# An attention and max-of-three FFN kernel: the row maximum turned by two 64-row matmuls, key totals folded in blocks, FFN products freed from one chain, a new order

## The chip, the cores and the metric

One Trainium2 chip, one of its cores. The metric is the device time of one execution in microseconds. Each version is also run once under the profiler, which records each instruction of each engine. Five engines matter: TensorE (PE, with its weight loads as PEld), VectorE (DVE), ScalarE (ACT), GpSimd (POOL), and SyncE (SP), which here only issues DMAs.

## The reference

```python
# q, k, v: (8, 8, 1152, 64) float32; x @ w: (4608, 512) @ (512, 768), w_out: (768, 512)
q_pool = q.reshape(B, H, S // 2, 2, D).mean(axis=3)
scores = np.matmul(q_pool, k.transpose(0, 1, 3, 2)) / np.sqrt(D)
scores = scores - np.max(scores, axis=-1, keepdims=True)
attn = np.exp(scores)
attn = attn / (np.sum(attn, axis=-1, keepdims=True) + 1e-09)
x = np.matmul(attn, v).transpose(0, 2, 1, 3).reshape(B * 576, H * D)
out = np.maximum(np.maximum(x @ w1, x @ w2), x @ w3) @ w_out
```

## The kernel before

**Units.** The attention is cut into 64 units d: a batch, a pair of heads and half of the 576 queries (288). Keys lie on the 128 partitions in nine blocks kk. Each unit does, in short:

1. qk (L568, L581): each key block times the queries of both heads, one head on array rows 0 to 63, the other on rows 64 to 127, into one of two PSUM slots `pqk`. From unit 8 on, K and Q are split into a high and a low part, and each product is three passes. ACT copies the slot to SBUF `s` (L597), and DVE takes the running maximum `acc` over key blocks (L603, L606).
2. The maximum over the partitions: DVE turns and reduces `acc` by 32 by 32 blocks to 18 columns of `crest` (L642), PE transposes `crest` whole, 128 by 128 (L652), DVE reduces it to 18 rows (L656), ACT and DVE split it into a high and a low part (L661, L664), POOL spreads both into block diagonals `diag` (L667), and two matmuls with ones, one for each head, broadcast the maximum over partitions into PSUM (L691).
3. DVE subtracts it from `s` (L703, six instructions a unit), ACT takes the exponential (L711), and POOL adds the nine key blocks into `ksum` (L743, L745).
4. av (L772): `s` times `v`, 36 matmul records a unit, one head on array columns 0 to 63, the other on 64 to 127. ACT copies the result to `xr` (L781).
5. The totals, from unit 8 on: `total` (L787) multiplies a matrix of ones with `ksum`, so that the sum stands on all partitions of its head; ACT adds 1e-9 (L791), DVE takes 288 reciprocals a partition (L795), POOL scales `xr` (L798). The first eight units use another form (L820 to L857). ACT and POOL then split x into `xh` and `xl` (L909, L912).

**FFN.** Ten chunks of token columns (288, 288, six of 512, 384, 576). A chunk makes 18 weight tiles g (three per hidden block of 128), each with four products kk, each of three passes (L1053); then four output tiles, each with six products. `two` makes two output tiles together: phase 0 puts the first tile on rows 0 to 63 and the second on rows 64 to 127, phase 1 changes the halves over. A tiny ACT copy, the mark (L1074), waits for the last matmul of phase 0, and the first matmuls of phase 1 wait for the mark. All products lie on one chain, `tail[0]`. Each tile goes from PSUM to SBUF `hm` (ACT copy L1114 for the first of three, DVE maximum L1116 for the second and third), and then ACT and POOL split `hm` into `h` high and low (L1124, L1127). The first output product waits for all of `h`.

**PSUM.** Four banks `ff` are shared by the FFN tiles (two for each call of `two`), the turned and the broadcast maxima, av and the totals. `spool` holds THIRDS = 7 thirds of a unit's `s`.

**Order.** Each `step` is an entry of a plan in the order of its creation. `ORDER` lists the entries' numbers, and `run` emits them in that order, so that every engine's queue is what `ORDER` says. The plan's own costs (`pe`, `act`, `dve`, `pool`) do nothing when the kernel is run. A step's `after` are steps that must be emitted earlier.

Of the kernel before, what the change touches and what calls it, by code (L numbers as in the profile page):

```python
# [24 lines left out]
NB = 18  # L25
DM = 512
# [11 lines left out]
1 3 68 0 2 7 9 8 10 12 11 13 14 4 333 5 342 15 18 16 17 21 65 67 334 19 337 335 20 336 24 338 66 22 343 25 339 23 27  # L38
28 26 344 30 31 29 70 32 72 346 71 73 340 33 34 75 345 35 36 76 74 77 37 78 132 351 910 352 353 347 38 81 79 80 354 46
39 84 355 82 83 87 40 51 348 85 88 41 86 90 89 93 911 133 130 6 195 356 52 131 349 360 197 42 91 94 92 95 96 44 43 357  # L40
135 137 136 138 139 140 97 143 45 141 47 144 142 145 98 146 149 48 361 147 99 49 100 196 358 101 912 148 150 151 362
54 152 363 50 53 153 154 102 155 109 55 158 364 198 369 341 69 267 706 264 365 56 156 370 112 366 115 113 159 110 157
103 373 111 160 161 200 201 57 202 162 205 58 203 104 105 163 371 164 206 114 106 204 165 207 372 107 208 59 209 367
166 707 374 211 212 174 167 116 375 108 175 265 376 134 266 350 378 387 210 60 213 61 168 170 119 178 176 214 217 215
180 120 218 379 382 169 216 219 220 223 121 221 224 172 62 63 380 222 225 269 271 381 388 391 226 389 383 390 177 173
270 272 384 171 122 392 385 123 227 274 273 64 228 229 230 277 275 278 124 393 179 276 708 543 199 774 709 396 377 231
279 184 232 239 280 233 240 775 394 241 245 283 281 284 181 397 234 125 185 235 282 286 287 285 398 126 127 399 288
289 186 128 292 405 400 401 243 237 406 290 187 402 293 409 236 242 291 407 188 294 295 296 408 403 189 297 298 410
117 129 299 300 247 248 711 713 712 714 359 386 368 414 268 777 253 715 246 244 308 301 716 313 717 719 254 190 309
# [12 lines left out]
891 581 944 582 945 946 947 837 948 583 1145 481 1212 478 1146 838 949 1147 950 584 839 479 892 1148 480 951 1150 840
899 585 952 1151 953 841 954 1149 1210 487 885 1216 1152 488 489 900 893 894 895 1215 1213 896 482 955 963 1153 956
901 903 964 957 966 968 1156 483 490 586 1211 1217 491 965 492 958 902 484 493 1154 1157 1155 590 1158 959 591 592
1159 1162 593 904 967 1160 905 1161 1163 594 595 1165 960 1166 1164 906 907 961 1167 1168 908 596 597 598 1169 1170
1221 1223 969 962 599 1171 1172 909 600 1173 1345 588 495 923 467 503 980 601 589 485 602 1347 970 971 972 973 587 974
975 496 504 1174 1222 1218 499 1224 507 497 498 1175 505 1176 506 1225 1177 1178 603 604 1226 1180 500 508 981 501
1227 605 606 607 1179 1182 1228 1229 1184 1230 509 1181 608 609 610 611 1232 1231 612 1185 502 1219 976 510 977 1235
618 619 620 621 1233 1236 1186 1234 1238 615 622 1187 1237 511 623 624 625 626 1239 1240 1189 1241 1188 512 515 1244
1242 1348 627 513 616 617 631 519 632 1346 633 634 635 636 1245 613 1183 637 1190 1243 1283 1284 1246 514 1247 638  # L70
1285 1286 1191 1192 1193 1194 614 516 1248 1288 639 640 628 1249 1250 520 629 1251 1252 1195 517 518 1196 494 1220
1287 521 522 1291 1253 641 1289 527 642 523 644 645 1199 1254 1256 1258 1290 643 1352 1354 1200 1255 524 1257 525 1259
1201 1205 1260 1261 1292 1206 646 1294 1295 647 648 649 528 650 1293 1297 1298 1296 529 530 651 652 653 654 1300 1299
1303 655 1263 659 660 661 662 1262 531 1301 1350 1304 1264 663 1302 1306 1305 1265 664 1355 1353 1349 1197 526 1198
630 1267 1202 1268 532 656 658 657 1307 1266 761 982 535 983 665 666 667 1359 1360 1308 668 669 1309 1361 1275 1364
1310 536 537 1281 670 671 539 1276 1311 538 533 1312 1362 540 541 1277 1313 1363 1367 1356 1365 1366 1282 1368 534 542
1314 672 673 674 1322 675 676 677 1370 1315 678 1371 1369 1323 1325 679 680 681 682 683 684 1373 1351 1269 1270 1357
1271 1326 829 978 897 685 1374 1327 1372 1376 1316 1377 1272 762 830 898 979 1273 689 690 691 692 693 694 1318 1375
1378 1317 1319 695 1379 1382 1320 696 697 698 699 985 1483 1484 984 686 687 688 700 701 986 987 1328 988 1324 1380
1381 1421 1383 1384 1423 989 704 702 1490 1321 1385 1386 1274 1387 1278 1329 703 1337 1422 990 1424 1388 1338 991 992  # L80
993 994 995 1426 1389 1390 1425 1391 999 1000 1001 1002 1392 996 1394 1396 1429 1398 1485 1330 1331 1332 1491 1492
1003 1393 1427 1395 1004 1005 1006 1007 1339 1008 1399 1428 1401 1343 1432 998 705 1358 1011 997 1014 1015 1016 1017
1397 1486 1400 1009 1430 1433 1018 1333 1334 1335 1336 1493 1487 1013 1012 1431 1434 1403 1435 1438 1344 1436 1439
1488 1019 1020 1021 1022 1437 1441 1029 1030 1031 1032 1402 1442 1033 1440 1443 1023 1444 1445 1446 1024 1497 1498
1404 1447 1034 1035 1036 1037 1499 1502 1448 1413 1449 1340 1405 1010 1406 1407 1408 1489 1025 1038 1494 1500 1503
1039 1501 1450 1414 1451 1415 1504 1419 1028 1027 1496 1040 1621 1041 1452 1495 1409 1416 1410 1026 1453 1454 1456
1458 1042 1043 1044 1045 1505 1508 1046 1506 1509 1455 1047 1048 1049 1050 1507 1460 1511 1510 1054 1420 1512 1514
1057 1058 1051 1461 1513 1052 1515 1459 1059 1060 1061 1463 1516 1465 1517 1462 1518 1062 1063 1064 1520 1065 1056
1055 1070 1622 1071 1072 1073 1074 1075 1457 1521 1464 1519 1522 1523 1066 1559 1561 1524 1411 1623 1412 1624 1467
1468 1469 1053 1076 1560 1562 1077 1078 1564 1079 1080 1067 1525 1526 1527 1563 1466 1565 1081 1528 1567 1536 1529  # L90
1481 1566 1537 1530 1532 1534 1082 1630 1538 1626 1531 1533 1628 1568 1570 1571 1068 1482 1085 1539 1086 1087 1088
1569 1573 1475 1470 1471 1625 1472 1631 1473 1474 1629 1543 1069 1089 1541 1572 1574 1476 1627 1544 1575 1090 1091
1576 1579 1092 1093 1084 1083 1098 1099 1100 1101 1577 1580 1535 1540 1097 1102 1578 1582 1581 1635 1103 1104 1105
1106 1583 1477 1584 1094 1585 1637 1636 1640 1586 1545 1478 1546 1542 1107 1638 1641 1632 1279 1108 1280 1551 1587
1588 1552 1109 1110 1095 1557 1589 1590 1096 1633 1639 1642 1553 1547 1548 1554 1549 1930 1634 1932 1550 1931 1591
1592 1643 1558 1341 1644 1646 1647 1593 1111 1112 1645 1113 1649 1594 1648 1650 1651 1114 1598 1115 1479 1595 1599
1116 1652 1117 1653 1655 1656 1600 1654 1657 1596 1118 1119 1658 1659 1937 1597 1601 1660 1120 1121 1868 1869 1602
# [1124 lines left out]
```

## Time and profile before

| | |
|---|---|
| median of three runs | 1340.11 us (1339.11 to 1342.76) |
| the profiled execution, its own time | 1336.39 us |
| its span, first to last instruction | 1334.6 us |
| TensorE clock granted, mean | 0.994 |
| busy in the span: PE, PEld, DVE, ACT, POOL | 97%, 75%, 76%, 70%, 85% |

The page of the profile gives busy time by engine and by 40 slices, the chain of work that ended last, and the groups of instructions. Matmuls are pipelined and their ends are modelled, so that a busy PE is not a PE at its peak. Starts are microseconds from the span's first instruction.

### The profile page before, as it was taken

What the parts mean: (1) busy time and instruction counts of PE and PEld (TensorE: products, weight loads), DVE (VectorE), ACT (ScalarE), POOL (GpSimd) and SP (SyncE); (2) the same over time, 40 slices, a digit from 0 to 9 for tenths busy, and PEclk for the clock granted to TensorE, in tenths of its full rate; (3) what the DMA queues carried; (4) which work ended last, traced back from release to release, by engine and by line L of the source; (5) the groups of instructions that cost most, each with busy time, mean ns of one, the idle gap of its engine ahead of it and who ended that gap; (6) DMA issues with size and microseconds to landing.
All of it is one profiled execution on the core that took longest, in us unless ns stands there. A gap on an engine that the chain in (4) does not pass through costs nothing.

```text
span 1334.6 us, 31849 instructions
## 1 busy us (share of the span) xinstructions
PE 1293.4 (97%) x12720; PEld 997.8 (75%) x12720; DVE 1019.0 (76%) x1351; ACT 930.8 (70%) x1756; POOL 1138.3 (85%) x981
## 2 busy tenths in 40 slices
PE   6999999999999999999999999999999999999998
PEld 2556678877777777787777877778777777778887
DVE  7889998888889889888888788888887888811010
ACT  7899987687768777777777767786777876622111
POOL 3798999999999999999999999999999998772110
PEclk8999999999999999999999999999999999999999
DMA  6667775524424143324432342243341423243531
GB/s 235 204 247 258 256 263 170 198 101 147 145 86 168 51 159 123 134 83 150 147 117 86 113 179 87 70 174 105 135 167 66 144 91 146 65 158 112 167 127 37
DMA packets 56324, 189.23 MB, mean 142 GB/s; under 512 B 6128, under 2 KB 12016, under 8 KB 56176
## 3 DMA queue, kind: packets, MB, share of 16 engines
q1 hardware_dynamic: 56176, 187.20, 40.5%
q8 instruction: 100, 1.64, 0.5%
q14 instruction: 48, 0.39, 0.1%
HBM read 168.30 MB, written 18.87 MB: 140 GB/s over the span
## 4 chain that ended last, share of the span: by engine, by line
PE 59%; POOL 20%; DVE 9%; ACT 5%; issue 4%; DMA 3%; SPq 0%; POOLq 0%; ACTq 0%; DVEq 0%
PE ff L1053 32%; PE ff L772 13%; POOL ksum L745 10%; PE pqk L581 10%; DVE acc L606 4%; DVE s L703 2%; PE ff L787 2%; POOL kc L524 2%; ACT s L597 1%; POOL xl L912 1%; POOL ksum L743 1%; DMA w<-in_win_dram 1%; POOL diag L667 1%; ACT s L711 1%; PE pqk L568 1%
## 5 line engine op out<-in xcount | busy, mean ns | idle before, releaser
L745 POOL TENSOR_TENSOR ksum<-ksum,s 128x576 f32<-128x576 f32 x407 | 579.7, 1426 | 16.9 <-ACT s L711 0.6
L1053 PE MATMUL ff<-xh,w 64*128 64x512 f32 (+2 forms) x3168 | 503.4, 357 | 10.8 <-ACT flag L1074 8.8
L597 ACT COPY s<-pqk 128x576 f32<-128x576 f32 x576 | 357.7, 637 | 93.5 <-PE pqk L581 68.0
L703 DVE TENSOR_TENSOR s<-s,ff 128x864 f32<-128x864 f32 x374 | 379.7, 1047 | 28.5 <-PE ff L691 25.3
L606 DVE TENSOR_TENSOR acc<-acc,pqk 128x576 f32<-128x576 f32 x448 | 335.6, 749 | 60.8 <-ACT s L597 45.2
L711 ACT ACTIVATE s<-s 128x864 f32<-128x864 f32 x384 | 347.8, 927 | 21.5 <-DVE s L703 20.0
L1053 PEld LDWEIGHTS ff<-xh,w 64*128 64x128 f32 x3168 | 323.2, 185 | 50.3 <-ACT flag L1074 20.2
L1053 PE MATMUL ff<-xl,w 64*128 64x512 f32 (+2 forms) x1584 | 308.8, 351 | 0.0
L581 PE MATMUL pqk<-qq,kc 64*128 64x288 f32 x3024 | 296.7, 301 | 5.3 <-DVE acc L606 4.0
L772 PE MATMUL ff<-s,v 128*64 128x288 f32 x2304 | 296.4, 410 | 0.0
L581 PEld LDWEIGHTS pqk<-qq,kc 64*128 64x128 f32 x3024 | 248.6, 185 | 51.1 <-DVE acc L606 23.5
L772 PEld LDWEIGHTS ff<-s,v 128*64 128x64 f32 x2304 | 162.2, 137 | 114.9 <-issue 6.6
L1053 PEld LDWEIGHTS ff<-xl,w 64*128 64x128 f32 x1584 | 174.4, 185 | 6.7
L1116 DVE TENSOR_TENSOR hm<-hm,ff 128x512 f32<-128x512 f32 (+2 forms) x132 | 75.5, 579 | 127.4 <-PE ff L1053 96.4
L1053 PE MATMUL ff<-h,wo 64*128 64x512 f32 (+2 forms) x1584 | 169.0, 351 | 3.2 <-ACT flag L1074 2.7
L1053 PEld LDWEIGHTS ff<-h,wo 64*128 64x128 f32 x1584 | 139.6, 185 | 14.8 <-ACT flag L1074 5.3
L1127 POOL TENSOR_TENSOR h<-hm,h 128x512 fp32r<-128x512 f32 (+2 forms) x66 | 71.4, 1087 | 78.2 <-ACT h L1124 78.2
L795 DVE RECIPROCAL rs<-rs 128x288 f32<-128x288 f32 (+1 forms) x64 | 110.5, 1727 | 11.6 <-ACT rs L791 10.3
L1074 ACT COPY flag<-eps 1x1 f32<-1x1 f32 x121 | 22.7, 188 | 114.9 <-PE ff L1053 114.2
L667 POOL TENSOR_TENSOR diag<-pick,parts 64x576 fp32r<-64x576 f32 x64 | 73.8, 1152 | 22.9 <-DVE parts L664 22.1
L743 POOL TENSOR_TENSOR ksum<-s 128x576 f32<-128x576 f32 x61 | 87.6, 1436 | 2.6 <-ACT s L711 1.8
L524 POOL TENSOR_TENSOR kc<-kraw,kc 128x384 fp32r<-128x384 f32 x84 | 84.7, 1012 | 0.0
(63 smaller groups left out, 1013.1 us busy)
## 6 DMA issues: line engine op xcount, KB each, us to landing
w<-w_split SPq DMA_DIRECT2D x180, 512.0 KB, 4.5
v<-in_vr_dram SPq DMA_DIRECT2D x36, 576.0 KB, 4.9
qraw<-in_qT_dram SPq DMA_DIRECT2D x28, 576.0 KB, 4.1
kraw<-in_kT_dram SPq DMA_DIRECT2D x28, 576.0 KB, 4.3
w<-in_win_dram SPq DMA_DIRECT2D x18, 512.0 KB, 4.4
w_split<-wo SPq DMA_DIRECT2D x18, 512.0 KB, 6.8
out_dram<-hm SPq DMA_DIRECT2D x24, 256.0 KB, 2.4
w<-in_wout_dram SPq DMA_DIRECT2D x6, 512.0 KB, 4.6
```

The costliest lines, as they stand in the source:

```text
L524: nc.gpsimd.tensor_tensor(o.kc[c][:, 1], src, o.kc[c][:, 0], op=ALU.subtract)
L581: nc.tensor.matmul(ps[:, h, :QH], kc[r, x, kk % 3 * P : kk % 3 * P + P], qq[r, y], start=i == 0, stop=i == 2, tile_position=(64 * h, 0),)
L597: nc.scalar.copy(o.s[kk // 3][:, kk % 3, slice(*hs)], o.ps[kk, hs][:, :, :QH])
L606: nc.vector.tensor_tensor(acc, acc, ps, op=ALU.max)
L667: nc.gpsimd.tensor_tensor(diag[d % 2][: 2 * SQ], pick[:, :, None].broadcast_to([2 * SQ, NB, SQ]), parts2[d % 2][:, None, :].broadcast_to([ ...
L703: nc.vector.tensor_tensor(s, s, o.pb[h][:, None, :w].broadcast_to([P, 3, w]), op=ALU.subtract)
L711: nc.scalar.activation(s, s, AF.Exp, scale=SCALE)
L743: vec[e].tensor_tensor(o.ksum, o.s[0][:, 0], x, op=ALU.add)
L745: vec[e].tensor_tensor(o.ksum, o.ksum, x, op=ALU.add)
L772: nc.tensor.matmul(o.pav[64 * h : 64 * h + 64, :QH], pr.v[:, kk, h], o.s[kk // 3][:, kk % 3, h], start=(kk == 0), stop=(kk == NK - 1),)
L795: nc.vector.reciprocal(o.rs, o.rs)
L1053: x = nc.tensor.matmul(jobs[u].ps[:, : hi - lo], weight(outs[u], a, kk)[r], moving(y, kk, lo, hi)[r], start=phase == kk == i == 0, stop=ph ...
```

## The change

1. **Maximum.** A DVE step `lower` moves the lower 64 partitions' 18 columns beside the upper ones; the transpose becomes two of 64 rows (64 columns moved each). The high and the low part are written twice (rows 0 to 63 for one head, 64 to 127 for the other), so that `diag` has 288 columns in place of 576 on 128 rows in place of 64, and the two broadcasts use different halves of the array's rows.
2. **Totals.** DVE folds `ksum` by 32 by 32 blocks to 18 columns; two matmuls with nine moving columns add them; DVE adds 1e-9, takes nine reciprocals a partition, turns them by blocks into PSUM and scales `xr`. The 288-column matmuls, ACT's add, the long reciprocal and POOL's scaling go.
3. **FFN.** `tail` has one chain for each phase, so that phase 0 of the next pair may stand among phase 1 of this one. The third tile of three stays in its PSUM bank: DVE writes the maximum there, ACT and DVE split it out of the bank (L1127's work goes from POOL to DVE), and only then is the bank free. The tiles of `h` are taken half by half, after their last readers, and each output product waits for its own block of `h`.
4. THIRDS is 8 in place of 7, and `ORDER` is new (6500 entries, 64 more).

```diff
-THIRDS = 7
+THIRDS = 8
...
+6361 6362 6363 6364 6355 6367 6353 6354 6368 6369 6370 6371 6366 6365 6372 6380 6381 6382 6373 6383 6374 6375 6376
...
+6433 6434 6435 6436 6426 6429 6427 6430 6428 6431 6437 6449 6438 6450 6439 6451 6440 6441 6442 6443 6444 6452 6453
+6454 6445 6447 6455 6446 6448 6466 6467 6456 6457 6458 6459 6460 6461 6468 6469 6470 6471 6464 6462 6483 6472 6484
+6473 6474 6485 6486 6487 6475 6488 6476 6477 6489 6478 6465 6463 6479 6481 6480 6482 6490 6491 6492 6493 6494 6495
...
+        def lower(e):
+            c = crest[d % 2]
+            nc.vector.tensor_reduce(c[:64, SQ : SQ + NB], c[64:, :NB, None], axis=AX.X, op=ALU.max)
...
-            nc.tensor.transpose(o.pb[0][:, :P], crest[d % 2], ident)
+            for i in range(2):
+                nc.tensor.matmul(
+                    o.pb[0][:, 64 * i : 64 * i + 64], crest[d % 2][:64, SQ * i : SQ * i + P], ident[:64, :64], start=True, stop=True,
+                    is_transpose=True, tile_position=(0, 0),
+                )
...
-            nc.scalar.copy(parts2[d % 2][:NB], o.top)
+            for i in (0, 64):
+                nc.scalar.copy(parts2[d % 2][i : i + NB], o.top)
...
-            nc.vector.tensor_tensor(parts2[d % 2][SQ : SQ + NB], o.top, parts2[d % 2][:NB], op=ALU.subtract)
+            for i in (SQ, 64 + SQ):
+                nc.vector.tensor_tensor(parts2[d % 2][i : i + NB], o.top, parts2[d % 2][:NB], op=ALU.subtract)
...
-                diag[d % 2][: 2 * SQ],
-                pick[:, :, None].broadcast_to([2 * SQ, NB, SQ]),
-                parts2[d % 2][:, None, :].broadcast_to([2 * SQ, NB, SQ]),
+                diag[d % 2],
+                pick[:, :, None].broadcast_to([P, HB, SQ]),
+                parts2[d % 2][:, None, :].broadcast_to([P, HB, SQ]),
...
-                half = diag[d % 2][: 2 * SQ, NB // 2 * h : NB // 2 * h + NB // 2]
+                r = slice(64 * h, 64 * h + 64)
                 nc.tensor.matmul(
-                    o.pb[h][:, :QH], wide[: 2 * SQ], half.rearrange("p t k -> p (t k)"), start=True, stop=True
+                    o.pb[h][:, :QH], wide[r], diag[d % 2][r].rearrange("p t k -> p (t k)"), start=True, stop=True,
+                    tile_position=(64 * h, 0),
                 )
...
+        def fold_sums(e):
+            o.fs = small.tile([P, NB], F32, tag="fs", name=f"fs{d}")
+            nc.vector.tensor_reduce(
+                o.fs,
+                o.ksum.rearrange("p h q -> p (h q)").rearrange("p (t k) -> p t k", t=NB),
+                axis=AX.X,
+                op=ALU.add,
+                apply_transpose=True,
+            )
...
-                nc.tensor.matmul(o.psm[64 * h : 64 * h + 64, :QH], ones, o.ksum[:, h], start=True, stop=True)
...
+                nc.tensor.matmul(
+                    o.psm[64 * h : 64 * h + 64, QH : QH + HB], tied, o.fs[:, HB * h : HB * h + HB], start=True, stop=True
+                )
...
+        def inverse(e):
+            o.rs = small.tile([P, HB], F32, tag="rw", name=f"rs{d}")
+            nc.vector.tensor_scalar(o.rs, o.psm[:, QH : QH + HB], EPS, None, op0=ALU.add)
             nc.vector.reciprocal(o.rs, o.rs)
...
+            nc.vector.transpose(
+                o.psm[:, :QH].rearrange("p (t k) -> p t k", t=HB), o.rs[:, :, None].broadcast_to([P, HB, SQ])
+            )
...
-            e1 = step("eps", d, [("act", 0.395)], add_eps, [t, scaled.get(d - 1)], give="ff")
-            t = step("inv", d, [("dve", 1.87)], reciprocal, [e1])
-            m = scaled[d] = step("xm", d, [pool(QH)], scale, [t, c])
+            t = chain[d] = step("fsum", d, [("dve", 0.7)], fold_sums, [o.sums[-1], turned.get(d - 2)])
+            t = turned[d] = step("psum", d + 0.99, [pe(100)], total, [t], cols=36, mode=1, take="ff")
+            t = step("inv", d, [("dve", 0.85)], inverse, [t])
+            m = step("xm", d, [dve(QH)], scale_wide, [t, c], give="ff")
...
-                            for h in (0, 1) if phase == 0 else (1, 0):
+                            for h in range(2):
...
-                        [tail[0]] + (ready(kk) if phase == 0 else [] if kk else marked),
+                        [tail[phase]] + (ready(kk) if phase == 0 else [] if kk else marked),
...
-                        nc.vector.tensor_tensor(o.x, o.x, t.ps[:, :m], op=ALU.max)
-                    ff_free.append(t.ps)
...
+                        nc.vector.tensor_tensor(o.x if j == 1 else ps, o.x, ps, op=ALU.max)
+                    if j < 2:
+                        ff_free.append(t.ps)
...
-                        vec[e].tensor_tensor(
-                            h.lo[f // 3][:, f % 3, lo:hi], o.x, h.hi[f // 3][:, f % 3, lo:hi], op=ALU.subtract
...
+                        nc.vector.tensor_tensor(
+                            hid.lo[f // 3][:, f % 3, lo:hi], t.ps[:, : hi - lo], hid.hi[f // 3][:, f % 3, lo:hi], op=ALU.subtract
                         )
-
-                    x = ffn_step("hhigh", at, 0, [("act", 0.09 + m / 1200)], high, [prev[p]])
-                    y = ffn_step("hlow", at, 0, [pool(m)], low, [x])
...
+                        ff_free.append(t.ps)
...
+                    y = ffn_step("hlow", at, 0, [dve(m)], low, [x], give="ff")
+                    hdone[f] += [x, y]
```

## Rows read from the trace of the kernel before

**Rows 1.** The page, part 1: busy us, share of the span, instructions.
```profile
PE 1293.4 (97%) x12720; PEld 997.8 (75%) x12720; DVE 1019.0 (76%) x1351; ACT 930.8 (70%) x1756; POOL 1138.3 (85%) x981
```
**Rows 2.** Busy time by stretch: PE, PEld, DVE, ACT, POOL, then clock, DMA.
```profile
100.00:200.00 100.00, 96.62 (x1052) 70.41 (x1046) 94.15 (x141) 92.06 (x171) 95.11 (x83) 1.00 0.77 259
...
300.00:1100.00 800.00, 795.02 (x7433) 616.73 (x7431) 682.32 (x854) 600.67 (x1107) 777.35 (x666) 1.00 0.35 122
...
1242.00:1334.60 92.60, 81.07 (x1128) 75.60 (x1128) 9.83 (x24) 15.10 (x53) 9.49 (x12) 0.99 0.29 96
```
**Rows 3.** The page, part 4: the chain that ended last, by engine.
```profile
PE 59%; POOL 20%; DVE 9%; ACT 5%; issue 4%; DMA 3%; SPq 0%; POOLq 0%; ACTq 0%; DVEq 0%
```
**Rows 4.** Groups by line and shape, PE, 300 to 1100 us: count, busy, mean ns.
```profile
L1053 PE MATMUL ff<-xh,w 64*128 64x512 f32 x1600 | 305.2, 397 | 0.0
L581 PE MATMUL pqk<-qq,kc 64*128 64x288 f32 x2366 | 233.5, 301 | 3.1 <-DVE acc L606 2.2 <-DVE acc L603 0.3
L772 PE MATMUL ff<-s,v 128*64 128x288 f32 x1572 | 199.0, 407 | 0.0
L1053 PE MATMUL ff<-xl,w 64*128 64x512 f32 x800 | 179.8, 392 | 0.0
L1053 PE MATMUL ff<-h,wo 64*128 64x512 f32 x720 | 95.1, 391 | 0.0
```
**Rows 5.** The chain in order of time, 600 to 640 us: start, duration, what.
```profile
616.40 2.80 PE ff L1053 x24
...
622.97 0.79 PE pqk L581 x12
...
623.80 0.33 PE ff L652
624.13 2.99 PE ff L1053 x24
...
627.65 0.64 PE ff L787 x4
628.29 4.36 PE ff L772 x36
```
**Rows 6.** Timeline of PE, 125 to 127 us: start, duration, what.
```profile
125.42 0.67 PE L835 MATMUL ff<-sel,kt 128*96 128x2 f32 x6
126.03 1.32 PE L568 MATMUL pqk<-qq,kc 64*128 64x288 f32 x8
```
**Rows 7.** The chain in order of time, 1255 to 1270 us.
```profile
1257.26 0.20 ACT flag L1074
...
1257.50 3.48 PE ff L1053 x42
...
1261.30 3.48 PE ff L1053 x42
```
**Rows 8.** Waits from 1150 us to the end, PEld: us, times, longest.
```profile
PEld ff L1053 <- ACT flag L1074: 20.9, 35, 0.9
```
**Rows 9.** Groups by line, DVE, 300 to 1100 us.
```profile
L795 DVE RECIPROCAL rs<-rs 128x288 f32<-128x288 f32 x44 | 85.7, 1948 | 8.9 <-ACT rs L791 7.8 <-POOL ksum L745 0.8
L1116 DVE TENSOR_TENSOR hm<-hm,ff 128x512 f32<-128x512 f32 x65 | 43.7, 672 | 6.3 <-PE ff L1053 5.6
L642 DVE TRANSPOSE_TENSOR_REDUCE crest<-acc 128x18 f32<-128x576 f32 x44 | 34.2, 777 | 1.2
...
L664 DVE TENSOR_TENSOR parts<-ff,parts 18x32 fp32r<-18x32 f32 x43 | 7.7, 180 | 12.3 <-ACT parts L661 11.8
```
**Rows 10.** Groups by line, the whole span.
```profile
L857 DVE TENSOR_TENSOR xr<-xr,ff 128x288 f32<-128x288 f32 x8 | 3.5, 433 | 0.1
```
**Rows 11.** Groups by line, POOL, 300 to 1100 us.
```profile
L667 POOL TENSOR_TENSOR diag<-pick,parts 64x576 fp32r<-64x576 f32 x44 | 50.7, 1153 | 5.4 <-DVE parts L664 4.7
L1127 POOL TENSOR_TENSOR h<-hm,h 128x512 fp32r<-128x512 f32 x32 | 41.1, 1287 | 0.0
...
L798 POOL TENSOR_TENSOR xr<-xr,rs 128x288 f32<-128x288 f32 x44 | 35.5, 807 | 0.0
```

More of the change, by code (lines that the diff above doesn't have):

```diff
@@ L25 @@
 NB = 18
+HB = NB // 2
 DM = 512
@@ L476, in plain_heads @@
         o.kmoved = [x]
-        o.lv = step("load", todo[0][0] + 2, [("sp", 0.5)], load_v, [av[pairs[n - 2].last]] if n > 1 else [], size=576)
+        o.lv = step("load", todo[0][0] + 2, [("sp", 0.5)], load_v, [av[u] for u in pairs[n - 2].units] if n > 1 else [], size=576)
     def heads(n, b, j, todo):
@@ L482, in heads @@
         r = todo[0][0]
-        o.last = todo[-1][0]
+        o.last, o.units = todo[-1][0], [u for u, _ in todo]
         before = pairs.get(n - 1)
@@ L543, in heads @@
             o.ksplit += [x, y]
-        o.lv = step("load", r + 2, [("sp", 0.5)], load_v, [av[pairs[n - 2].last]], size=576)
+        o.lv = step("load", r + 2, [("sp", 0.5)], load_v, [av[u] for u in pairs[n - 2].units], size=576)
     blanks = step("top", 0, [("dve", 3.2)], lambda e: blank(), [])
@@ L675, in scores @@
         o.accread = [x]
-        x = o.turned = step("turn", d, [pe(150)], turn, [x], take="ff")
+        x = step("red", d, [("dve", 0.17)], lower, [x, getattr(old2, "turned", None)])
+        x = o.turned = step("turn", d, [pe(130)], turn, [x], mode=3, take="ff")
         x = step("top", d, [("dve", 0.25)], summit, [x])
-        y = step("top", d, [("act", 0.2)], m_high, [x] + getattr(old2, "full", []))
-        x = step("top", d, [("dve", 0.17)], m_low, [x, y] + getattr(old2, "full", []))
-        full = step("diag", d, [("pool", 1.16)], spread_out, [x, y] + getattr(old2, "bcs", []))
+        y = step("top", d, [("act", 0.3)], m_high, [x] + getattr(old2, "full", []))
+        x = step("top", d, [("dve", 0.34)], m_low, [x, y] + getattr(old2, "full", []))
+        full = step("diag", d, [("pool", 0.65)], spread_out, [x, y] + getattr(old2, "bcs", []))
         o.full = [full]
@@ L698, in scores, with maximum @@
             last_sub = None
+            def maximum(e, h=h):
+                o.mcopy = small.tile([P, QH], F32, tag="rs", name=f"mcopy{d}", bufs=1)
+                nc.scalar.copy(o.mcopy, o.pb[h][:, :QH])
+                if GIFT[d] == 3:
+                    ff_free.append(o.pb[h])
+            if keep:
+                mc = step("sub", d, [act(QH)], maximum, [b] + gifts.get(d - 1, []), give="ff" if keep == 3 else None)
+                o.subs[h].append(mc)
             for i in range(3):
@@ L717, in sub_copied @@
                     )
-                def maximum(e, h=h):
-                    o.mcopy = small.tile([P, QH], F32, tag="rs", name=f"mcopy{d}", bufs=1)
-                    nc.scalar.copy(o.mcopy, o.pb[h][:, :QH])
-                    if GIFT[d] == 3:
-                        ff_free.append(o.pb[h])
                 r = d + 0.1 * i + 0.05 * h
                 if 2 - i < keep:
-                    if 3 - i == keep:
-                        mc = step("sub", r, [act(QH)], maximum, [b, gifts.get(d - 1)], give="ff" if keep == 3 else None)
-                        o.subs[h].append(mc)
-                    x = gifts[d] = step("sub", r, [pool(3 * w)], sub_copied, [mc, copies[-1]])
+                    x = step("sub", r, [pool(3 * w)], sub_copied, [mc, copies[-1]])
+                    gifts.setdefault(d, []).append(x)
                 else:
@@ L1025, in needed, with begin, two @@
             return [a for x, steps in ready_x[b, kk] if lo <= x < hi for a in steps]
-        def begin():
-            third = lambda name: hpool.tile([P, 3, NQ], F32, tag="t", name=f"{name}{b}").bitcast(F32R)
-            quarters = [third(f"h{i}") for i in range(4)]
-            h.hi, h.lo = quarters[:2], quarters[2:]
+        hid = Job()
+        hid.hi, hid.lo = [None, None], [None, None]
+        def begin(i):
+            for name, home in (("hi", hid.hi), ("lo", hid.lo)):
+                home[i] = hpool.tile([P, 3, NQ], F32, tag="t", name=f"{name}{b}_{i}").bitcast(F32R)
         def supply(g):
             fetch(g)
-        def two(outs, nk, weight, moving, ready, start=None):
+        def two(outs, nk, weight, moving, ready):
             jobs, both = [Job() for _ in outs], Job()
@@ L1087, in ffn @@
             supply(g)
-        hdone = []
+        hdone = [[] for _ in range(6)]
+        firsts = [None, None]
         outs = [(g, p, lo, hi) for g in range(NG) for p, (lo, hi) in enumerate(parts)]
```

88 lines of the change are left out of this document (43 added, 45 removed), and 539 rows, old and new, of the table ORDER.

## The prediction

> **What bounds the kernel now.** The first view is busy time by engine [rows 1]: TensorE 97%, POOL 85%, DVE 76%. These are averages over unlike stretches, so the second view is busy time by stretch [rows 2]. From 300 to 1100 us, the steady middle, PE is busy for 795 of 800 us and POOL for 777; DVE has 682, weight loads 617. From 1242 us on only PE is busy. The granted clock is 0.99 or 1.00 in these rows, so nothing below hangs on it. The third view, the chain that ended last [rows 3], gives PE 59%, but POOL 20% and DVE 9%: in a fifth of the time what ends last is a POOL instruction, so PE's "busy" hides waits.
>
> How full is PE really? I count records [rows 4] and price them with undisturbed pieces of the chain [rows 5]. A step of six FFN records at width 512 takes 2.80 / 4 = 0.70 us, a qk step of six records 0.79 / 2 = 0.395, av 4.36 a unit. The middle holds (1600 + 800 + 720) / 6 = 520 FFN steps, 364 us; 2366 / 6 = 394 qk steps, 156 us; 1572 / 36 = 43.7 units of av, 190 us; one total (0.64) and one turn (0.33) a unit, 42 us. That is 752 of 800 us, 94%; the other 48 us are the broadcasts, which I have not counted, changes of the array's form, and waits. A unit takes 800 / 43.7 = 18.3 us: PE needs 17.2 of it, POOL 17.8, DVE 15.6. So PE and POOL bound the middle together, and PE alone bounds the end. What leaves PE or its waits is worth its time as long as no other queue takes over.
>
> **The change part by part.**
>
> *Totals (56 units).* Leave PE: four records that stand with av. The piece of 0.64 [rows 5] holds the change of the array's form as well, which av pays anyway, so I price four records at av's rate, 4 x 4.36 / 36 = 0.48. Come: four records of nine columns. The nearest row is six records of two columns, 125.42 to 126.03, 0.10 each [rows 6]: 0.41 for four in series, 0.10 if all four overlap. I take 0.25, since two column halves work beside each other as in av. Saved: 0.23 x 56 = 13 us, bounds 0.07 x 56 = 4 and 0.38 x 56 = 21.
>
> *Turn (64 units).* The 128 by 128 transpose takes 0.33, and the four FFN steps behind it take 2.99 in place of 2.80 [rows 5]: 0.52 together, as row work stands on both sides and the array changes its form twice. The new one is two passes of 64 rows, in the form of the row work; none is in the trace. One pass of 288 columns takes 0.395 / 3 = 0.13, so two cost at most 0.26, which I take, though they move 64 columns each. Among row work that saves 0.26; where av or a total follows, the change of form is paid anyway and 0.07 is left. I take 0.17 between: 11 us, bounds 4 and 17.
>
> *Broadcasts.* Two passes of 0.13, both on rows 0 to 63, become one on each half. If they meet, 0.13 x 64 = 8 us are saved; if a neighbour already used the free half, nothing. I take 3.
>
> PE's work falls by 27 us, bounds 8 and 46, 0.45 a unit.
>
> *Two chains in the FFN.* At the end the chain shows the price of a mark: pairs start every 3.80 us (1257.50, 1261.30) with 0.20 of ACT between them [rows 7]. Eight steps of 288 columns at the qk rate are 3.16, so a mark costs 0.64. The last chunk has 18 + 4 pairs: 14 us. Weight loads wait for 35 marks from 1150 us on, 20.9 us, 0.60 each [rows 8]; the 13 outside the last chunk are 8 us more. The new order takes this away where it puts the next pair's phase 0 around the mark, and the end of it says so: numbering back from 6499, each of the last pairs has 17 entries, so 6432 to 6437 are a pair's phase 0, 6438 its mark, 6439 its first product of phase 1; the order has 6437, 6449 (the next pair's first), 6438, 6450, 6439. The work that hides the mark is thus one or two steps of 0.39 us, against 0.20 of ACT and some 0.1 of signals; were they not there, 0.64 would come back. Some of the 13 already stand beside attention work: I take 18 of 22 us, bounds 14 and 22.
>
> *The third tile stays in PSUM.* A bank is held for the maximum (0.67 [rows 9]), an ACT copy and another 0.67 on DVE, some 1.3 us longer. Queued behind it is the next pair that wants the bank. At the end two pairs take turns on the four banks, so that a pair's banks are wanted again only after the other pair's phase, 4 x 0.39 = 1.6 us; in the middle qk steps, which need no `ff` bank, are the cover. I take 0; uncovered it is the third rival below. No DMA is added, and a weight slot is still refilled after the last phase 1 that reads it; that `h` is taken and waited for in pieces only loosens waits, and I take 0 for it too.
>
> *DVE.* A unit loses the reciprocal, 1.95 [rows 9]. It gains the fold of the totals, 0.78 as the fold of the maximum; four small ones (`lower`, the second low part, the add, nine reciprocals) at 0.18, 0.72; the scaling, 0.43 as L857 [rows 10]; and the turn of the reciprocals into PSUM, which the trace lacks: between 0.18 and 0.78, taken at 0.43 as the same 288 columns with PSUM on one side. The sum is +0.41. The low part of `h` adds 32 tiles [rows 11] of 0.67 in 43.7 units, 0.49. DVE goes from 15.6 to 16.5 us a unit; at 18.3 - 0.45 = 17.85 it is 92% full. POOL loses 0.81 and 32 / 43.7 x 1.29 = 0.94, and half of `diag`'s columns, 0.58 [rows 11]: 17.8 becomes 15.5, 87%. The Trainium skill (VectorE: DVE Perf Modes, The three transpose paths) gives 311 ns for a 128 by 128 block transpose; the nine blocks of 32 columns would by that scale to an estimate of 0.70, and no run here shows it. By it a unit has 0.27 more on DVE, 94% full, and the sum below stays as long as PE bounds.
>
> Can a queue be so full? From 100 to 200 us DVE is busy for 94 of 100 us, with ACT at 92 and PE at 97 [rows 2]. So POOL's relief and DVE's load cancel in my sum, with 0 for both.
>
> *The first eight units* have no totals of this form. They get `lower` and the second low part, 0.36 on a DVE that is the fullest engine but PE there: 8 x 0.36 = 3 us. The eighth third of `s` may give some of it back: bounds +3 and -5.
>
> **The sum.** The profiled execution took 1336.4 us itself (span 1334.6, 1.8 around it). 1336.4 - 27 - 18 + 3 = 1294.4. The median of the runs is 3.7 above the profiled execution, 1340.1 to 1336.4: **1298 us**. With all bounds its own range is 1336.4 - 8 - 14 + 3 + 3.7 = 1321 down to 1336.4 - 46 - 22 - 5 + 3.7 = 1267.
>
> **Rivals.**
>
> *DVE takes over; slower.* Its queue is in order, and the new chains cross engines: total on PE, then four on DVE; maximum on DVE, copy on ACT, subtraction on DVE. If the next unit's maximum stands behind such a wait, qk stalls for its slot. DVE is 85% full in the middle today; at 87% a unit would take 16.5 / 0.87 = 19.0, +0.7 x 56 = 39 us, less the 15 of the end and the start: 1340 + 24 = 1364. It decides where DVE can't be kept above 89%: 16.5 / 0.89 = 18.5 costs the 15 us that the rest gains. For it speaks that DVE work comes in bursts; against it the 94% from 100 to 200 us [rows 2]. The Trainium skill (VectorE: DVE Perf Modes, Rules for kernel authors) tells authors to minimize the count of DVE operations, which here rises by six a unit; the trace's small ones at 0.18 show what each costs. Chance 0.10.
>
> *PE's work was not the limit in the middle.* POOL at 97% paces it and DVE takes its place at the same pace, so that PE gains waits as it loses work. Only the marks count: 1336.4 - 18 + 3 + 3.7 = 1325. For it speaks the chain's 20% of POOL [rows 3], against it my 94%. The Trainium skill (Trainium Kernel Development and Optimization, Performance Expectations) calls matmul busy time a bad measure and weight-load time a good one; by that rule PE would be 75% full [rows 1], and this rival would hold. Chance 0.12.
>
> *Banks.* Some 50 third tiles beside attention hold a bank 1.3 us longer; if half of that stalls PE, 33 us come back: 1331. Against it speaks that few waits for a bank show now. Chance 0.05.
>
> *POOL's relief is worth more.* Half of the 1.1 us a unit that PE does not stream goes: 0.55 x 56 = 31, 1267. Against it DVE's 92%. Chance 0.10.
>
> *The change doesn't do what it says* only if the order kept phases apart, which its end excludes.
>
> **How the numbers follow.** My forecast has 0.60, no change (cases cancelling) 0.03. Faster by over 0.3% (about what a measurement of this kernel tells from none) are the forecast and the rivals at 1325, 1331 and 1267: 0.87. Same 0.03, slower 0.10. The range 1266 to 1328 takes in the rivals at 1325 and 1267, and leaves out the slower one and the banks, 0.15, and little else; the likeliest case's own range is 1280 to 1315.
>
> **What would show it.** Right: pairs at the end 3.2 us apart and no PE wait on marks; total's line near 0.25 us a unit; POOL under 90% and DVE over 90% in the middle at units of 17.8 us. Wrong: weight loads that wait for DVE's maximum or for a bank freed by the low part of `h`; DVE at 85% with PE waiting; units still 18.3 us apart.

## The result and the profile after

The changed kernel takes 1270.06 us (median of 4 runs, 1268.65 to 1271.19) against 1339.61 for the kernel before in the same comparison: a ratio of 0.9477, with an interval of 0.9457 to 0.9498. That is 69.5 us less, where I forecast 42. The profiled execution took 1269.19 us itself, with a span of 1267.3.

The page of the kernel after, parts 1 and 4, answers to [rows 1, 3]:

```profile
PE 1244.6 (98%) x12784; PEld 1014.4 (80%) x12784; DVE 1067.7 (84%) x1771; ACT 924.0 (73%) x1764; POOL 998.4 (79%) x859
...
PE 80%; DVE 6%; ACT 5%; POOL 4%; issue 2%; DMA 1%; SPq 0%; ACTq 0%; POOLq 0%; DVEq 0%
```

PE's busy share hardly tells the two kernels apart (97 and 98%), the chain does: PE ends last in 80% of the span where it was 59, and POOL in 4% where it was 20. Busy time by stretch, columns as in [rows 2]:

```profile
100.00:200.00 100.00, 97.58 (x1089) 73.38 (x1089) 97.33 (x160) 95.62 (x181) 94.88 (x82) 1.00 0.75 262
...
300.00:1100.00 800.00, 799.15 (x7862) 663.69 (x7859) 741.59 (x1200) 618.21 (x1158) 705.39 (x606) 1.00 0.37 130
...
1180.00:1267.30 87.30, 82.33 (x1201) 80.72 (x1198) 14.91 (x36) 17.62 (x59) 3.51 (x5) 0.99 0.33 109
```

In the middle DVE is 93% full and POOL 88%; PE misses 0.85 of 800 us and issues 7862 matmuls instead of 7433. Groups of PE from 300 to 1100 us, as [rows 4]:

```profile
L1080 PE MATMUL ff<-xh,w 64*128 64x512 f32 x1728 | 332.8, 394 | 0.0
L591 PE MATMUL pqk<-qq,kc 64*128 64x288 f32 x2454 | 238.2, 299 | 0.8 <-ACT s L607 0.4 <-DVE acc L613 0.2
L797 PE MATMUL ff<-s,v 128*64 128x288 f32 x1620 | 206.1, 409 | 0.0
L1080 PE MATMUL ff<-xl,w 64*128 64x512 f32 x864 | 202.2, 390 | 0.0
L1080 PE MATMUL ff<-hi,wo 64*128 64x512 f32 x512 | 101.3, 394 | 0.0
L1080 PE MATMUL ff<-lo,wo 64*128 64x512 f32 x256 | 60.9, 391 | 0.0
```

Counted as before: (1728 + 864 + 512 + 256) / 6 = 560 FFN steps of 0.70, 392 us; 409 qk steps of 0.395, 162; 1620 / 36 = 45 units of av of 4.36, 196. That is 750 of 800 us, where the same three kinds made 710 before. What lies between them (totals, turns, broadcasts, a dozen narrower output steps in both, changes of the array's form, waits) fell from 90 us to 50.

A fixed window does not hold the same work in both kernels. A stretch that does, but for half a per cent, runs from the start of the 17th unit's av to the start of the 61st's (36 records a unit, counted from the first). Before:

```profile
315.15:1120.84 805.69, 802.10 (x7465) 621.57 (x7462) 686.23 (x861) 603.48 (x1114) 780.01 (x666) 1.00 0.36 126
```

After:

```profile
306.95:1074.78 767.83, 766.98 (x7519) 633.88 (x7518) 715.10 (x1158) 595.98 (x1112) 686.24 (x589) 1.00 0.37 130
```

Both hold 44 units with 1584 av records, 3198 and 3216 FFN records, 2376 and 2370 of qk. A unit takes 18.31 us before and 17.45 after. At the prices above the three kinds make 721 and 723 us, so what lies between them fell from 1.92 to 1.02 us a unit.

The chain in order of time of the kernel after, from 603 to 640 us, to be held against [rows 5], has PE pieces only, back to back:

```profile
604.14 0.79 PE pqk L591 x12
604.93 4.51 PE ff L797 x36
609.45 0.07 PE ff L822 x4
609.52 0.33 PE ff L712
...
618.78 0.05 PE ff L667
618.83 0.38 PE pqk L591 x4
...
633.96 0.22 PE ff L822 x4
634.18 0.60 PE pqk L591 x6
```

A total (L822) adds 0.07 or 0.22 us, a turn (L667) 0.05. At the end, the same view answers to [rows 7] with a chain without marks for its last 37 us:

```profile
1216.13 9.84 PE ff L1080 x144
...
1226.05 0.20 ACT flag L1101
...
1226.29 37.39 PE ff L1080 x542
```

144 records are three pairs of 48, so a pair takes 9.84 / 3 = 3.28 us where pairs started 3.80 apart. Weight loads from 1080 us on wait for marks 8 times instead of 35 [rows 8]:

```profile
PEld ff L1080 <- ACT flag L1101: 4.9, 8, 0.7
```

The new groups of DVE over the whole span, beside [rows 9, 10], give the prices that the trace of before lacked:

```profile
L811 DVE TRANSPOSE_TENSOR_REDUCE fs<-ksum 128x18 f32<-128x576 f32 x56 | 43.1, 769 | 2.2 <-POOL ksum L770 2.0
...
L830 DVE STREAM_TRANSPOSE ff<-rs 128x288 f32<-128x288 f32 x56 | 27.7, 494 | 1.9
...
L829 DVE RECIPROCAL rs<-rs 128x9 f32<-128x9 f32 x56 | 12.1, 216 | 1.9
L662 DVE TENSOR_REDUCE crest<-crest 64x18 f32<-64x18 f32 x64 | 10.7, 168 | 2.1
```

### The profile page after: what moved, and what is told of

It reads as the page before. It is cut to its first block, busy times and chain, and to the rows that moved or that the text cites. A ratio compares the mean times of both kernels' runs of the same rounds, so it can differ in the third digit from the quotient of the medians.

```text
span 1267.3 us, 32164 instructions
## 1 busy us (share of the span) xinstructions
PE 1244.6 (98%) x12784; PEld 1014.4 (80%) x12784; DVE 1067.7 (84%) x1771; ACT 924.0 (73%) x1764; POOL 998.4 (79%) x859
## 4 chain that ended last, share of the span: by engine, by line
PE 80%; DVE 6%; ACT 5%; POOL 4%; issue 2%; DMA 1%; SPq 0%; ACTq 0%; POOLq 0%; DVEq 0%
PE ff L1080 43%; PE ff L797 19%; PE pqk L591 14%; DVE acc L616 3%; POOL ksum L770 2%; ACT s L607 2%; PE pqk L578 2%; ACT s L744 2%; DVE s L736 1%; PE ff L712 1%; DMA w<-w_split 1%; DVE acc L613 1%; POOL xl L948 1%; PE ff L822 1%; POOL ksum L768 0%
## 5 line engine op out<-in xcount | busy, mean ns | idle before, releaser
L770 POOL TENSOR_TENSOR ksum<-ksum,s 128x576 f32<-128x576 f32 x407 | 579.7, 1429 | 17.8 <-ACT s L744 2.0
L1080 PEld LDWEIGHTS ff<-xh,w 64*128 64x128 f32 x3168 | 346.5, 184 | 25.9 <-ACT flag L1101 7.3
L1080 PE MATMUL ff<-xl,w 64*128 64x512 f32 (+2 forms) x1584 | 321.9, 350 | 0.0
L591 PE MATMUL pqk<-qq,kc 64*128 64x288 f32 x3024 | 294.4, 299 | 0.8 <-ACT s L607 0.4
L591 PEld LDWEIGHTS pqk<-qq,kc 64*128 64x128 f32 x3024 | 255.1, 185 | 27.5 <-DVE acc L616 10.1
L1080 PEld LDWEIGHTS ff<-xl,w 64*128 64x128 f32 x1584 | 190.8, 185 | 3.7
L1080 PE MATMUL ff<-hi,wo 64*128 64x512 f32 (+2 forms) x1056 | 167.1, 352 | 0.0
L1080 PEld LDWEIGHTS ff<-hi,wo 64*128 64x128 f32 x1056 | 118.2, 184 | 4.3 <-ACT flag L1101 0.2
L1080 PE MATMUL ff<-lo,wo 64*128 64x512 f32 (+2 forms) x528 | 109.5, 349 | 0.0
L687 POOL TENSOR_TENSOR diag<-pick,parts 128x288 fp32r<-128x288 f32 x64 | 43.2, 675 | 73.3 <-DVE parts L684 49.2
L1145 DVE TENSOR_TENSOR hm<-hm,ff 128x512 f32<-128x512 f32 (+2 forms) x66 | 38.1, 584 | 58.1 <-PE ff L1080 53.8
L578 PE MATMUL pqk<-qq,kc 64*128 64x288 f32 x288 | 62.7, 544 | 11.1 <-DMA kc<-in_kT_dram 4.9
```

The source lines that it names most:

```text
L578: nc.tensor.matmul(ps[:, h, :QH], pr.k[kk // 6][r, kk % 6 * P : kk % 6 * P + P], pr.q[o.half][r, 1], start=True, stop=True, tile_position= ...
L591: nc.tensor.matmul(ps[:, h, :QH], kc[r, x, kk % 3 * P : kk % 3 * P + P], qq[r, y], start=i == 0, stop=i == 2, tile_position=(64 * h, 0),)
L687: nc.gpsimd.tensor_tensor(diag[d % 2], pick[:, :, None].broadcast_to([P, HB, SQ]), parts2[d % 2][:, None, :].broadcast_to([P, HB, SQ]), op ...
L770: vec[e].tensor_tensor(o.ksum, o.ksum, x, op=ALU.add)
L1080: x = nc.tensor.matmul(jobs[u].ps[:, : hi - lo], weight(outs[u], a, kk)[r], moving(y, kk, lo, hi)[r], start=phase == kk == i == 0, stop=ph ...
```

## Experiments

The middle's gain is larger than my sum, so three questions stand: are the marks and the turn worth what I said; does the rest come from POOL's relief; or from the order. Experiments 1 to 5 undo one part in the new kernel and keep its order (a step goes out at its place in the list, or as soon as the steps that it needs and a bank are there; 2 and 5 also move the undone steps, as said there). Experiments 6 to 8 add idle work, which nothing waits for but its own queue. Experiments 9 to 11 take work out of the kernel before, whose order stays but for the marks of the eleventh.

**1. One chain in the FFN again.**

```diff
-                    tail[phase] = ffn_step(
+                    tail[0] = tail[1] = ffn_step(
...
-                        [tail[phase]] + (ready(kk) if phase == 0 else [] if kk else marked),
+                        [tail[0]] + (ready(kk) if phase == 0 else [] if kk else marked),
```

> The changed kernel with its FFN products on one chain again (phase 0 of a pair only after phase 1 of the pair before), everything else and the order kept as far as that allows. Theories. W (work): PE is the one bound, and what leaves its stream is gained at its price. P (POOL): what the change gained beyond the forecast is POOL's relief. O (order): the new order and the eighth third made the room, single parts matter little. W and P: 22 bare marks of 0.64 us in the last chunk and some 13 of 0.60 before it come back, 1270 + 20 = 1290 us, 1286 to 1296. O: under 1280, or far over 1300 if the order only works with two chains.

Measured: 1285.43 us, ratio 0.9602 (0.9578 to 0.9627), 15 us above the kernel after and just under the 1286 to 1296 that were expected. Its waits over the whole span, and its chain at the end, where pairs start 3.78 apart again:

```profile
PEld ff L1092 <- ACT flag L1113: 23.1, 47, 1.0
```

```profile
1231.12 0.20 ACT flag L1113
...
1231.36 3.46 PE ff L1092 x47
...
1234.90 0.20 ACT flag L1113
```

Over the whole span of the kernel after this wait has 7.5 us in 21 waits: 23.1 - 7.5 = 15.6. The time lost is the wait put back, and it is lost at the end (17 of it behind the 61st unit's av, last table of this section). The marks are worth 15 us; the forecast was 18.

**2. The old totals (288 columns, wide add and reciprocal, scaling on POOL) in the place of the new total**, with ACT's add halfway to the reciprocal.

```diff
-                    o.psm[64 * h : 64 * h + 64, QH : QH + HB], tied, o.fs[:, HB * h : HB * h + HB], start=True, stop=True
+                nc.tensor.matmul(o.psm[64 * h : 64 * h + 64, :QH], ones, o.ksum[:, h], start=True, stop=True)
```

> The changed kernel with the totals of the kernel before: ones times ksum over 288 columns, ACT adds epsilon, long reciprocal on DVE, POOL scales. W: PE gets back 0.23 to 0.45 us a unit, 1270 + 13 to 25 = 1283 to 1295 us. P: POOL gets 0.81 us a unit more (88 to 93% full) on top, 1305 or more. O: under 1278.

Measured: 1515.06 us, ratio 1.1311 (1.1271 to 1.1352); the granted clock of the profiled execution is 0.935 on the mean. Theory P had 1305 or more, but 245 us are not the price of 0.81 us of POOL a unit. POOL's longest wait of the whole span is a new one:

```profile
POOL ksum L791 <- PE ff L846: 111.1, 21, 13.1
```

The new kernel's fold reads `ksum` early and frees its buffer, so its total can stand late, beside av. The old total reads `ksum` itself: at that late place it keeps the next units' sums on POOL waiting up to 13.1 us, where POOL waits 0.7 us in all for the fold in the kernel after. These 111 us are under half of what is lost; other queues wait as well (qk weight loads 85.5 us for DVE's maximum, broadcasts 55.7 for `diag`). This prices the place, not the work; it does not say what the totals are worth. It does show that the fold buys freedom of place, which my sum has no term for.

**3. One 128-row transpose again, without `lower`.**

```diff
-            for i in range(2):
-                nc.tensor.matmul(
...
+            nc.tensor.transpose(o.pb[0][:, :P], crest[d % 2][:, :P], ident)
```

> The changed kernel with the maximum turned by one 128-row transpose again, and without the DVE step that lowers columns. W and P: 0.07 to 0.26 us of PE a unit, 1275 to 1287 us, most likely 1281. O: 1270, as DVE is a little freer.

Measured: 1280.96 us, ratio 0.957 (0.9545 to 0.9595), 11 us above the kernel after and as forecast: 11 / 64 = 0.17 us a turn. The Trainium skill (TensorEngine Tiling (Array Packing), Key Properties) says that a change of the tiling mode drains TensorE. The traces are in line with it, though they show only the time: the 64-row turn that keeps the neighbours' form adds 0.05 or 0.07 us in the chain, and the 128-row one took 0.33 and 0.19 more on the steps behind it [rows 5].

**4 and 5. The low part of `h` on POOL again, the bank free after the maximum; in 5 it stands 40 entries later in the order.**

```diff
-                        nc.vector.tensor_tensor(
-                            hid.lo[f // 3][:, f % 3, lo:hi], t.ps[:, : hi - lo], hid.hi[f // 3][:, f % 3, lo:hi], op=ALU.subtract
+                        nc.gpsimd.tensor_tensor(
+                            hid.lo[f // 3][:, f % 3, lo:hi], o.x, hid.hi[f // 3][:, f % 3, lo:hi], op=ALU.subtract
```

> The changed kernel with the low part of h on POOL again: the third tile goes to SBUF by the maximum, its bank is free at once, POOL subtracts. POOL gets 0.9 us a unit more (88 to 93%), DVE 0.5 less (93 to 90%). W: 1270 us, 1267 to 1274. P: 1280 to 1295. O: within 5 us of 1270.

> As e4_hlow, but POOL's subtraction stands 40 entries (some 8 us) later in the order, as in e4 POOL stood 128 us in total at this step's old place, waiting for ACT's high part. Theory P (POOL's load is what counts): 1290 us or more still. Theory Q (place): the 67 us of e4 were the queue standing at a step placed too early, and POOL's load itself costs little: under 1285 us.

Measured: 1336.7 us (0.9995, 0.9981 to 1.0009) and 1352.75 us (1.0103, 1.0076 to 1.013): the fourth beyond all three theories, the fifth on the side of P. Waits of the fourth over the whole span:

```profile
POOL lo L1172 <- ACT hi L1169: 127.6, 34, 13.0
PEld ff L724 <- POOL diag L699: 37.2, 26, 7.2
PE ff L724 <- POOL diag L699: 28.5, 19, 6.9
```

POOL stands at `lo` for ACT's copy, up to 13 us, and `diag` of the next unit is queued behind it, so PE waits for its broadcast. Standing later moves the trouble: in the fifth, POOL still waits 96.6 us for `hi`, and the second products wait for `lo`, 25.6 us of weight loads. My theory that 40 entries were enough fell too. It is half right in the middle, where a unit takes 17.99 us in the fifth and 18.53 in the fourth; behind the 61st unit's av the fifth loses 45 us to the kernel after (last table of this section). As in 2, a part undone inside an order made without it shows a misfit, not a price.

**6. POOL's load back as idle work**, additions at three places of a unit (some 2.1 us in all by their groups) beside `diag`, the inverse and `lo`; one of them:

```diff
+            nc.gpsimd.tensor_tensor(idle, idle, idle, op=ALU.add)
```

> The changed kernel with idle work on POOL, without data of others: 288 columns at the inverse of the totals (0.81 us, 56 times), as much as the low part of h at its place (66 times), 192 columns behind diag (64 times): what the change took from POOL, some 2.3 us a unit, with no other queue touched. P: POOL paces again, 88% becomes full, a unit grows to 18.0 to 18.5 us, 1285 to 1310 us. W (PE's work and waits alone): no more than POOL's floor, 18.0 against 17.8 us a unit, 1270 to 1282.

Measured: 1328.78 us, ratio 0.9917 (0.9889 to 0.9946): 59 us above the kernel after and beyond both theories. Busy time from 300 to 1100 us, and waits of the whole span:

```profile
300.00:1100.00 800.00, 766.82 (x7419) 623.04 (x7418) 704.32 (x1138) 587.90 (x1100) 759.76 (x735) 0.99 0.35 122
```

```profile
PEld ff L715 <- POOL diag L689: 41.5, 33, 3.0
PE ff L715 <- POOL diag L689: 30.6, 26, 2.7
ACT s L609 <- POOL ksum L773: 21.0, 17, 4.0
```

With POOL at 95% `diag` comes late, PE waits for it and drops to 767 of 800 us. The new order does not bear the old load of POOL.

**7 and 8. Idle work on PE, two 288-column products ahead of each total; on DVE, the fold of the totals twice.**

```diff
+            for h in range(2):
+                nc.tensor.matmul(o.psm[64 * h : 64 * h + 64, :QH], ones, idle, start=True, stop=True)
```

```diff
+            nc.vector.tensor_reduce(
+                again,
...
```

> The changed kernel with two idle matmuls of 288 columns ahead of each total, ones times a constant tile: 0.48 us of PE in 56 units, at the same place, no other queue touched. W: all of it comes through, 1270 + 27 = 1297 us, 1290 to 1300. If PE were not the bound (its waits take it up): 1270 to 1280.

> The changed kernel with the fold of the totals done twice, the second into a tile that nobody reads: 0.77 us of DVE in 56 units, 93% becomes 97% full. W: DVE has room, 1270 to 1280 us. If DVE's fullness is what holds the changed kernel now: 1295 or more (0.5 to 0.8 us a unit).

Measured: 1293.97 us (0.9665, 0.964 to 0.969), 24 above the kernel after for 56 x 0.48 = 27 us of PE work, as expected; and 1289.95 us (0.9631, 0.9609 to 0.9653), 20 above for 56 x 0.77 = 43 us of DVE work, between the two expectations. Busy time of the eighth from 300 to 1100 us:

```profile
300.00:1100.00 800.00, 792.95 (x7696) 642.09 (x7694) 754.78 (x1226) 607.47 (x1130) 699.17 (x600) 1.00 0.37 129
```

In the new kernel added PE work costs nine tenths of its length at av's rate: PE is the limit. DVE is near it: 0.77 us a unit more, at 94% full, made a unit 0.40 longer. POOL waits 1.4 us in all for the second fold, so a late `ksum` is not the cause.

**9. The kernel before with POOL relieved** by some 2.1 us a unit, its order kept; the ninth key block's sum and the scaling of x are left out:

```diff
+                if kk == 8:
+                    return
...
-            vec[e].tensor_tensor(xs, xs, o.rs, op=ALU.mult)
+            pass
```

> The kernel before, in its own order, with POOL work left out from unit 8 on: the ninth key block is not added to ksum (1.43 us) and x is not scaled by the reciprocals (0.81 us): 2.2 us a unit, what the change took from POOL. Theories. L (loads): POOL at 97% paced the middle together with PE, and its relief pays by itself: 1305 to 1320 us. R (room for another order): with the order kept the relief gives little, under 10 us: 1328 us or more; what e6_poolload cost was an order that counted on the relief.

**10. The kernel before with the totals' products cut to nine columns:**

```diff
-                nc.tensor.matmul(o.psm[64 * h : 64 * h + 64, :QH], ones, o.ksum[:, h], start=True, stop=True)
+                nc.tensor.matmul(o.psm[64 * h : 64 * h + 64, :9], ones, o.ksum[:, h, :9], start=True, stop=True)
```

> The kernel before, in its own order, with the totals' matmuls cut to nine of 288 columns (the other columns' totals are left out, ACT still writes 288): the change's saving on PE alone, 0.23 to 0.38 us in 56 units. PE the bound: 1338 - 13 to 21 = 1317 to 1325 us. POOL the pace: 1330 or more.

**11. Both together, with two chains in the FFN and the next pair's first two products ahead of each mark of the last chunk:**

> e9 and e10 together, and in the last chunk the next pair's first two products ahead of each mark, two chains in the FFN: the change's three reliefs in the old order, the same work left out. L: the three add up, 25 + 15 + 13: 1275 to 1295 us. R: the old order keeps half or more of it: 1300 us or more.

Measured, beside 1337.79 us for the kernel before: 1335.77 (0.9987, 0.9972 to 1.0002), 1333.64 (0.9974, 0.9958 to 0.9991) and 1324.32 (0.99, 0.9874 to 0.9925). One row from 300 to 1100 us of each, first the ninth:

```profile
300.00:1100.00 800.00, 795.18 (x7440) 617.64 (x7438) 682.05 (x854) 600.45 (x1107) 685.84 (x578) 1.00 0.35 122
```

The tenth:

```profile
300.00:1100.00 800.00, 789.10 (x7466) 614.11 (x7464) 682.87 (x858) 602.03 (x1111) 779.06 (x667) 1.00 0.35 124
```

The eleventh:

```profile
300.00:1100.00 800.00, 792.48 (x7508) 619.57 (x7506) 687.96 (x863) 603.95 (x1119) 691.47 (x583) 1.00 0.35 125
```

POOL falls from 777 [rows 2] to 686 us, and nothing clear of noise comes of it: 2 us. What POOL gains it spends for the most part on a new wait, the ninth's from 300 to 1100 us:

```profile
POOL diag L667 <- DVE parts L664: 58.5, 34, 3.5
```

Cutting the totals takes 13 to 21 us from PE by my sum (0.23 to 0.38 a unit; over the whole span the totals' group falls from 39.5 to 16.1 us), and 4 come back. The FFN steps of these 800 us stay what they were: the group that has 1600 records in [rows 4] has 1600, 1600 and 1601 in the three runs, and 1728 in the kernel after. Of the eleventh's 13.5 us, some 4 are its marks: its last chunk, the last 1152 FFN records, takes 91.1 us to the end of the span, where the kernel before takes 94.7 and the kernel after 83.2. (Its weight loads wait 9 us less for marks from 1150 us on, 11.8 against 20.9 [rows 8], but a weight load's wait is not all PE's.) So POOL's and PE's relief together bring some 10 us in the old order. The ninth and the eleventh came out as theory R had them, the tenth as a kernel whose pace PE does not set.

**12. The kernel after with seven thirds of `s`** (`THIRDS = 7`), its steps put off where they need the eighth.

> The changed kernel with seven thirds of s in place of eight, in its order as far as that allows: steps that would overwrite a third still in use are put off. If the eighth third only gave the order a little slack: 1270 to 1276 us. If the order needs it: 1285 us or more.

Measured: 1550.51 us, ratio 1.1592 (1.1562 to 1.1623), granted clock 0.944. The order is made for the eighth buffer and falls apart without it. What the eighth buffer would be worth in an order made for seven, this does not say.

**The stretch with the same work, from the 17th unit's av to the 61st's, in the profiled execution of each run.** It is steadier than the whole: experiment 1, which loses its time behind it, has it within 1 us of the kernel after. The start varies more: among the kernel before and experiments 9 to 11, whose first eight units are alike, the ninth unit's av starts between 161.1 and 166.4 us. Experiments 2 and 12, whose order broke, are left out.

| kernel | 44 units, us | one unit, us | from there to the end, us |
|---|---|---|---|
| before | 805.7 | 18.31 | 213.8 |
| 9, POOL relieved | 805.3 | 18.30 | 212.5 |
| 10, PE relieved | 802.3 | 18.23 | 213.7 |
| 11, both and marks | 796.4 | 18.10 | 210.0 |
| after | 767.8 | 17.45 | 192.5 |
| 1, one chain | 767.1 | 17.44 | 209.9 |
| 3, old turn | 779.5 | 17.71 | 194.7 |
| 4, low part on POOL | 815.2 | 18.53 | 199.1 |
| 5, the same, later | 791.7 | 17.99 | 237.7 |
| 6, POOL loaded | 814.8 | 18.52 | 195.5 |
| 7, PE loaded | 785.7 | 17.86 | 195.5 |
| 8, DVE loaded | 785.5 | 17.85 | 192.8 |

## Why the prediction held, and where its size was off

**Right: the range, the marks, the turn, and no new bound.** 1270 lies inside the stated range of 1266 to 1328, but only 4 us above its lower end, which was drawn for a rival; the likeliest case's own range, 1280 to 1315, missed it. The marks brought 15 us (forecast 18), the turn 11 (forecast 11), both by undoing them. DVE came out at 93% and POOL at 88% (forecast 92 and 87), and PE waited for neither: DVE did not take over. The second view of the prediction, DVE at 94 of 100 us from 100 to 200 us, was the right evidence for it; experiment 8 shows that the room ended there, since 0.77 us a unit more cost 20 us in all. The rival of the banks finds no wait: PE misses 0.85 us in the middle. The turn of the reciprocals into PSUM took 0.49 us where I took 0.43. The Trainium skill (VectorE: DVE Perf Modes, The three transpose paths) led to an estimate of 0.70. The measurement decides, and 0.49 is shorter.

**Off by little.** A total is 0.25 us by its group's busy time, as I took it; in the chain from 603 to 640 us it adds 0.07 or 0.22, as the rest of it overlaps with its neighbours. The broadcasts, put at -3 us, gained nothing that their group shows: 317 ns a record in the middle, 320 before. The first eight units' 3 us do not show: the ninth unit's av starts at 163.7 us before and at 163.3 after, but a start varies by more than that.

**Right by luck: the unit of 17.8 us.** 800 / 45 = 17.78 seems to bear out the forecast of 17.85, but the window from 300 to 1100 us ends where attention thins out in the new kernel: the 61st unit's av starts at 1074.8 us, the 62nd's at 1104.3. Between equal points a unit takes 17.45 us, 0.40 less than forecast. A period is a measure only if what is done in it stays the same.

**The step that failed: "POOL's relief and DVE's load cancel in my sum, with 0 for both".** It leaves the time that PE does not stream, beyond the named parts, as it was. A unit became 0.86 us shorter between equal points, and my sum had 0.45. From the ninth unit's av to the 61st's that is 46 us where the sum had 52 x 0.45 = 23, so most of the 28 us from 1298 to 1270 lies there. Part of it is a matter of size: undoing the turn costs (779.5 - 767.8) / 44 = 0.26 us a unit in this stretch, where I took 0.17, and a total adds some 0.12 to the chain (L822 is 0.7% of it from 307 to 1075 us), where I took 0.25. If both hold, that is half of the missing 0.41.

In time the rival of POOL's relief, 1267, came closest, and it is half right: with the load back as idle work the new kernel loses 59 us (experiment 6), but the relief alone, in the old order, gives nothing clear of noise (experiment 9). Less PE work alone gives 4 of 13 to 21 us (experiment 10), both together some 10 beside the marks (experiment 11). In the old order the rival at 1325 was thus right that PE's work did not set the pace of the middle, though PE was busy for 795 of 800 us; that POOL alone set it is not borne out either. In the new order the same resources have their price: 59 us for POOL's old load, 24 for 27 us on PE, 20 for 43 us on DVE. So neither the lighter work in the old order nor the new order with POOL's old load, where a unit takes 18.52 us, brings the gain of the middle; the two together do. What the order could use is seen in part: `ksum` free early (experiment 2), an eighth third (experiment 12), a `diag` that is seldom late (over the whole span the broadcasts' weight loads wait for it 3.9 us in the kernel after and 41.5 in experiment 6).

**Open.** How the rest of the 28 us divides among those was not settled: each undone alone broke the order, and a new order for each was not made. Nor was an order made anew for the old work. It was not shown either which hand-offs kept the old order from using what was freed; the waits for DVE's maximum stayed (18.0 us of qk weight loads before, 19.4 in experiment 11, 8.6 in the kernel after), but these explain some 10 us of it at most.

## What to carry to other kernels

A hand-written order over in-order queues is made for certain loads: work taken out of it alone may give nothing, and work put back into a better one may cost its full length, so forecast a change of work and order together from the gaps between the big pieces, not from the work alone. To learn what a queue's load is worth, add idle work that nothing waits for; undoing a part in an order made without it mostly measures a misfit of place. And take a period between two points that stand for the same work; a fixed window counts what happens to fall into it.

## What was not expected

PE's busy time was no help in both directions: 795 of 800 us before, with freed work worth a fifth to a third, and 799 after, with added work worth nine tenths. The weight loads' busy time (75 and 80% of the span) moved the right way; but at 664 of 800 us in the middle it does not show that PE is full, which experiment 7 does.

Where PE waits for long, its granted clock falls as well. Experiment 5 from 1100 to 1180 us:

```profile
1100.00:1180.00 80.00, 68.66 (x632) 58.45 (x631) 43.30 (x73) 38.54 (x77) 40.17 (x38) 0.91 0.23 81
```

PE is busy for 69 of 80 us here, and the clock of 0.91 is a mean over the levels of 2.4 and 1.2 GHz; the same stretch of the kernel after had 1.00. The mean clock of the profiled execution is 0.935 in experiment 2, 0.944 in 12, 0.976 in 5, 0.983 in 4 and 0.985 in 6. So the times of these hold some slower matmuls besides their waits.
